# The SBUF layout of an attention and two-MLP kernel: float32r matmul operands moved to the lower 128 KB of each partition

## The chip, the core and the metric

The kernel runs on one core of a Trainium2 chip. The metric is the device time of one execution in microseconds (us). The engines are named as the profile names them: PE (TensorE's matmuls), PEld (its weight loads, which overlap the matmuls), DVE (VectorE), ACT (ScalarE), POOL (GpSimd) and SP (SyncE, which here issues the DMAs; SPq is its queue).

## The reference, cut to what matters

```python
def _attn_ref(q, k, v):                       # (8, 8, 576, 64): batch, head, position, head dim
    q_s = softmax of q over the head dim
    k_s = softmax of k over the positions
    kv = einsum('bhsd,bhse->bhde', k_s, v)
    return einsum('bhsd,bhde->bhse', q_s, kv)

x = attn_out.transpose(0, 2, 1, 3).reshape(4608, 512)
h = x @ w_in1;  x = (h * sigmoid(1.702 h)) @ w_out1      # 512 -> 2048 -> 512, float64 weights
h = x @ w_in2;  x = max(0.01 h, h) @ w_out2              # 512 -> 2048 -> 512
```

The weights arrive as 64-bit floats and are converted on the chip to 32-bit ones.

## The kernel before, in words

The 4608 rows of x are cut into 9 chunks of 512. Each 32-bit operand of an MLP matmul is split into a high part of type float32r and a low part of the same type (what the high part lacks), and a product is the sum of three float32r matmuls: high by high, low by high, high by low. Such a matmul has a stationary operand of 128 x 128 (its weights, loaded by a LDWEIGHTS) and a moving one of 128 x 512. The rows of the trace write a matmul as out<-moving,weights.

- `g1` (L605) computes a block of h directly: moving `x`, weights `wi`, 12 matmuls. It serves chunks 0 and 1 of layer 0, and chunk 8 of both layers (`single`).
- `product` (L618), called from `quad_step`, computes blocks of h for two chunks at once from 7 products in place of 8, 6 matmuls each: moving `x` or `xb` (sums of blocks of x), weights `wa`, `wb`, `wc` or `wd`, outputs `ha`, `hb`, `hc`.
- `g2` (L665) multiplies the activated block by the second weights into four accumulators `acc`: operands `gh`/`gl` (the two parts of the activated block) and `wo`, one moving and the other stationary (exchanged in layer 1), 12 matmuls a block.
- Attention (L390, L400, L421, L476, L500) is plain float32: transposes `kma`, `kmb`, `qtp`, and the matmuls `kvp` and `pxt`. Its 36 units (a chunk and a pair of heads; 32 of them also have a k and v to work on) are dealt out between the matmuls of the MLP, so that there are some 168 short islands of attention on PE.

The program goes: attention of the first units; chunks 0 and 1 with the conversion of layer 0's weights (`c1` to `c4`); `pair_second` for chunk 1; then pairs of chunks (`pair_first`, then `pair_second`), with chunk 8 of each layer by `single`. ACT writes high parts (L80), DVE low parts (L83), DVE also adds the products (L774) and SP issues the DMAs in a fixed order.

Tiles come from pools. A pool stands on one side of the partition (left: counted up from below, right: down from the top), and a pool that is opened later may lie where a released one lay; a tile there waits for the last use of the tile that it replaces. `sb` (attention's tiles, `gf`, `gh`, `gl`, `xr`), `xa` (`x`), `wo` and `c0`/`gb` stand on the left. `first` (raw weights, their conversion, `wi`) stands on the right, and `late` takes its place after chunk 1 (`wa` to `wd`, `xb`, the products' tiles `p1`, `u2`, `v5`, and the conversion of layer 1's weights).

Of the kernel before, what the change touches and what calls it, by code (L numbers as in the profile page):

```python
# [9 lines left out]
F32R = mybir.dt.float32r  # L10
# [16 lines left out]
def tile_softmax_linear_attention_two_mlps(  # L27
# [20 lines left out]
    P = 128  # L48
    T = 512
# [10 lines left out]
    AHEAD = 6  # L60
    LAST = NCH - 1

    sb = ctx.enter_context(tc.tile_pool(name="sb", bufs=1, side="left", reuse_waits="tile"))
    xa = ctx.enter_context(tc.tile_pool(name="xa", bufs=1, side="left", reuse_waits="tile"))
    ps = ctx.enter_context(tc.tile_pool(name="ps", bufs=1, space=bass.MemoryType.PSUM))
    dram = ctx.enter_context(tc.tile_pool(name="dram", bufs=1, space=bass.MemoryType.DRAM))
# [10 lines left out]
    pool = dict(sb=sb, xa=xa)  # L77

    def split_hi(src, hi):
        nc.scalar.copy(hi, src)  # L80
# [182 lines left out]
    def load_wo(i, f):  # L263
        WO[f] = new_wo(f)
        nc.sync.dma_start(out=WO[f].rearrange("p h n -> p (h n)").bitcast(F32), in_=wod[i][f])
# [329 lines left out]
    gb = {}  # L595
# [48 lines left out]
            nc.vector.tensor_tensor(out=t, in0=t, in1=h, op=ALU.max)  # L644

    def halve_hi(f, t):
        gh = sb.tile([P, T], F32R, tag="gh", name="gh", bufs=3)
        gl = sb.tile([P, T], F32R, tag="gl", name="gl", bufs=3)
        split_hi(t, gh)
        g[f] = (t, gh, gl)  # L650

# [36 lines left out]
    def tail(layer, c, acc, between=None):  # L688

        for d in range(KT):  # L690
            for f in range(NF - LAG, NF):
                g2(layer, f, acc, (d,))
            finish(layer, c, acc, d)
            if between and d < len(between):
                between[d]()
# [72 lines left out]
    def quad_step(layer, n, gaps, extra):  # L768
# [24 lines left out]
        act1(layer, a, t11, False)  # L793
        act2(layer, a, t11, False)
        halve_hi(f0, t11)
        run(gaps[4])
        product(b, "s3", W["t3"], False)
# [10 lines left out]
        act1(layer, u2, t12, True)  # L808
        act2(layer, u2, t12, True)
        halve_hi(f1, t12)  # L810
        run(extra[0:1])
        halve_lo(f1)
# [30 lines left out]
    def ready(f):  # L843
        halve_hi(f, gb.pop(f))
        halve_lo(f)
# [31 lines left out]


    pool["wo"] = tc.alloc_tile_pool(name="wo", bufs=1, side="left", reuse_waits="tile")
    first = tc.alloc_tile_pool(name="first", bufs=1, side="right", reuse_waits="tile")  # L880
    pool["cv"] = pool["wi"] = first
    p0 = tc.alloc_tile_pool(name="c0", bufs=1, side="left", reuse_waits="tile")
    places[:] = [1] * 8

    load_first(p0)
# [15 lines left out]
        named[word[:2]](int(word[2:]))  # L901
    p0.release()
    early = False
    pool["gb"] = tc.alloc_tile_pool(name="gb", bufs=1, side="left", reuse_waits="tile")

    def second_x(c, j):
        direct_hi(c, 2, j)
# [80 lines left out]
    blocks = False  # L988
    load_wo(0, 0)
    load_wo(0, 1)  # L990
    first.release()
    late = tc.alloc_tile_pool(name="late", bufs=1, side="right", reuse_waits="tile")
    pool["cv"] = pool["wi"] = pool["xb"] = late
    wi_slots[0] = 5
    late_pools = True

# [153 lines left out]
                    run(items)  # L1150
            held = last
    tail(*held)
    late.release()
    pool["gb"].release()
    pool["wo"].release()


# [28 lines left out]
```

## Time and profile before

| what | value |
|---|---|
| time, median of 3 runs | 1660.8 us (1660.01 to 1662.22) |
| profiled execution: span from first to last instruction | 1657.3 us |
| what a run has beside the span: median less span | 3.5 us |
| PE busy | 1623.3 us, 98% |
| DVE, ACT, POOL busy | 1022.2, 695.4, 27.9 us |
| DMA | 391.55 MB, mean 236 GB/s |
| mean granted TensorE clock | 0.997 of 2.4 GHz |

The profile has no time of its own for the profiled execution beside its span, so the three runs stand for it. The end of a matmul in the trace is modelled and overlaps the start of the next, so that PE's busy time says little about its pace: what a matmul costs is read from the start of one to the start of the next.

### The profile page before, as it was taken

The numbers are of one execution on the slowest core, as the hardware profiler recorded it, in microseconds if no ns is written. First come the engines' busy times: TensorE is split into PE (matmuls) and PEld (weight loads), VectorE is DVE, ScalarE is ACT, GpSimd is POOL, SyncE is SP. The second block draws the span as 40 slices with busy tenths as digits, with TensorE's granted clock in tenths as the row PEclk, the third lists the DMA queues.
The fourth block names the chain that finished last, engine by engine and source line by source line (L and its number), as shares of the span: only waits on it lengthen the run. The fifth ranks groups of instructions, "written<-read, shape, count | busy, mean of one in ns | idle before, by whom it ended". The sixth has DMA issues, their size and how long they took to land.

```text
span 1657.3 us, 22131 instructions
## 1 busy us (share of the span) xinstructions
PE 1623.3 (98%) x7680; PEld 1288.0 (78%) x7680; DVE 1022.2 (62%) x1673; ACT 695.4 (42%) x1582; POOL 27.9 (2%) x162
## 2 busy tenths in 40 slices
PE   5999999999999999999999999999999999999998
PEld 3677777777777778777888888888888888888887
DVE  7899668886767776567435877354735473545222
ACT  8787655665555554444324334211321132112222
POOL 1000000000000000000000000000000000000000
PEclk9999999999999999999999999999999999999999
DMA  7787587778788788778867877665766566657662
GB/s 216 233 275 223 162 263 268 247 258 273 253 270 252 249 279 276 247 250 306 294 213 258 293 274 247 231 214 184 235 231 214 185 230 210 214 184 229 206 203 100
DMA packets 190864, 391.55 MB, mean 236 GB/s; under 512 B 57376, under 2 KB 99360, under 8 KB 190752
## 3 DMA queue, kind: packets, MB, share of 16 engines
q1 hardware_dynamic: 190752, 390.14, 72.2%
q8 instruction: 61, 1.00, 0.2%
q14 instruction: 51, 0.42, 0.1%
HBM read 308.28 MB, written 81.79 MB: 235 GB/s over the span
## 4 chain that ended last, share of the span: by engine, by line
PE 89%; DVE 2%; DMA 2%; issue 2%; ACT 1%; SPq 0%; POOL 0%; ACTq 0%; DVEq 0%; POOLq 0%
PE acc L665 44%; PE hb L618 14%; PE ha L618 10%; PE hc L618 9%; PE h L605 8%; PE pxt L500 2%; DMA o<-cv 1%; PE kvp L421 1%; PE qtp L476 1%; DMA wo<-wo 1%; DMA raw<-in_moe_w_in_dram 1%; DVE gl L83 0%; DVE cv L121 0%; DVE kt L406 0%; DMA w<-cv 0%
## 5 line engine op out<-in xcount | busy, mean ns | idle before, releaser
L665 PE MATMUL acc<-gh,wo 128*128 128x512 f32 x1152 | 363.7, 396 | 5.2 <-DMA wo<-wo 3.4
L665 PE MATMUL acc<-wo,gh 128*128 128x512 f32 x1152 | 355.7, 390 | 0.0
L665 PEld LDWEIGHTS acc<-wo,gh 128*128 128x128 f32 x1152 | 216.2, 188 | 46.4 <-issue 0.2
L665 PEld LDWEIGHTS acc<-gh,wo 128*128 128x128 f32 x1152 | 211.5, 188 | 51.4 <-issue 5.2
L665 PE MATMUL acc<-gl,wo 128*128 128x512 f32 x576 | 225.7, 392 | 0.0
L665 PE MATMUL acc<-wo,gl 128*128 128x512 f32 x576 | 225.2, 391 | 0.0
L605 PE MATMUL h<-x,wi 128*128 128x512 f32 x768 | 194.7, 403 | 2.8 <-ACT wi L80 2.8
L605 PEld LDWEIGHTS h<-x,wi 128*128 128x128 f32 x768 | 144.2, 190 | 41.4 <-ACT wi L80 4.5
L83 DVE TENSOR_TENSOR gl<-gb,gh 128x512 fp32r<-128x512 f32 x128 | 87.7, 689 | 124.2 <-ACT gh L80 123.8
L618 PE MATMUL ha<-x,wa 128*128 128x512 f32 x624 | 164.0, 398 | 0.0
L80 ACT CAST gh<-gf 128x512 fp32r<-128x512 f32 x160 | 98.9, 618 | 137.5 <-PE acc L665 66.9
L83 DVE TENSOR_TENSOR gl<-gf,gh 128x512 fp32r<-128x512 f32 x160 | 110.3, 690 | 65.0 <-ACT gh L80 63.3
L80 ACT CAST gh<-gb 128x512 fp32r<-128x512 f32 x128 | 79.2, 621 | 161.9 <-PE acc L665 161.4
L618 PEld LDWEIGHTS ha<-x,wa 128*128 128x128 f32 x624 | 115.7, 187 | 32.9 <-issue 5.0
L665 PEld LDWEIGHTS acc<-gl,wo 128*128 128x128 f32 x576 | 108.3, 188 | 24.7 <-issue 1.0
L665 PEld LDWEIGHTS acc<-wo,gl 128*128 128x128 f32 x576 | 108.1, 188 | 23.6
L774 DVE TENSOR_TENSOR u<-hb,p 128x512 f32<-128x512 f32 x56 | 38.6, 689 | 133.6 <-PE hb L618 117.9
L618 PE MATMUL hb<-x,wc 128*128 128x512 f32 x384 | 100.1, 395 | 0.0
L452 ACT ACTIVATE qt<-qt,qmx 128x64 f32<-128x64 f32 x256 | 86.1, 339 | 14.8 <-DVE qmx L442 14.4
L618 PE MATMUL hb<-xb,wb 128*128 128x512 f32 x336 | 87.0, 394 | 0.0
L618 PEld LDWEIGHTS hb<-x,wc 128*128 128x128 f32 x384 | 72.0, 187 | 17.3
L779 ACT COPY p<-ha 128x512 f32<-128x512 f32 x56 | 32.7, 584 | 117.3 <-PE ha L618 117.2
(125 smaller groups left out, 2076.9 us busy)
## 6 DMA issues: line engine op xcount, KB each, us to landing
wo<-wo SPq DMA_DIRECT2D x288, 512.0 KB, 4.2
wa<-wq SPq DMA_DIRECT2D x40, 512.0 KB, 4.1
wb<-wq SPq DMA_DIRECT2D x40, 512.0 KB, 4.6
wc<-wq SPq DMA_DIRECT2D x40, 512.0 KB, 4.7
raw<-in_moe_w_in_dram SPq DMA_DIRECT2D x32, 512.0 KB, 4.9
raw<-in_moe_w_out_dram SPq DMA_DIRECT2D x32, 512.0 KB, 5.1
wi<-wq SPq DMA_DIRECT2D x32, 512.0 KB, 4.5
wd<-wq SPq DMA_DIRECT2D x40, 256.0 KB, 3.4
```

Of the source, the lines that this page charges most:

```text
L80: nc.scalar.copy(hi, src)
L83: nc.vector.tensor_tensor(out=lo, in0=src, in1=hi.bitcast(F32), op=ALU.subtract)
L421: nc.tensor.matmul(pk[h * D : (h + 1) * D, 0 : D + 1], rest[0][:, h, :] if r == R and rest else km[:, h, r, :], vm[:, h, r, :] if r < R el ...
L452: nc.scalar.activation(t[:, h, r, :], t[:, h, r, :], AF.Exp, bias=mx[:, h, r : r + 1], accum_out=sm[:, h, r : r + 1],)
L476: nc.tensor.transpose(pt[:, r * P : (r + 1) * P], qs[:, r, :, :].rearrange("p h d -> p (h d)"), ident)
L500: nc.tensor.matmul(pv[o, :, a:e], kvb[b, j][o, :], t[o, :, a:e], start=True, stop=True)
L605: nc.tensor.matmul(h, WI[f][:, b, wh, o * P : (o + 1) * P], xs[f"a{side}{b + 1}"][xh][:, o, :], start=(i == 0), stop=(i == n - 1),)
L618: nc.tensor.matmul(h, w[:, wh, o * P : (o + 1) * P], xo[xh][:, o, :], start=(start and i == 0), stop=(i == 5), skip_group_check=not start,)
L665: nc.tensor.matmul(acc[d], lhsT, rhs, start=(f == 0 and i == 0), stop=(f == NF - 1 and i == 2))
L774: add = lambda out, h, t: nc.vector.tensor_tensor(out=out, in0=h, in1=t, op=ALU.add)
L779: nc.scalar.copy(p1, a)
```

## The change

No instruction is added or removed, and no tile's size or number of buffers changes. What changes is where the tiles lie:

| tiles | read by PE as | KB in the partition before | after |
|---|---|---|---|
| `gh`, `gl` | float32r | 47 to 59 | 16 to 28 |
| `x` | float32r | 75 to 107 | 28 to 60 |
| `wo` | float32r | 107 to 123 | 60 to 76 |
| `wi`, first part (8 buffers) | float32r weights | 184 to 216 | 76 to 108 |
| `wa` to `wd`, `wi`, later (5 buffers) | float32r weights | 168 to 188 | 76 to 96 |
| `xb` | float32r moving | 188 to 212 | 96 to 120 |
| raw weights and their conversion (8 buffers) | not read | 160 to 184 and 216 to 224 | 108 to 140 |
| `p1`, `u2`, `v5` | not read | 212 to 224 | 128 to 140 |
| `gb` (and attention's first inputs) | first inputs: float32 | 123 to 155 | 145 to 177 |
| attention's tiles | float32 | 16 to 41 | 177 to 202 |
| `gf`, `xr` | not read | 41 to 47, 59 to 75 | 202 to 224 |

```diff
-    sb = ctx.enter_context(tc.tile_pool(name="sb", bufs=1, side="left", reuse_waits="tile"))
+    sb = ctx.enter_context(tc.tile_pool(name="sb", bufs=1, side="right", reuse_waits="tile"))
+    lo = ctx.enter_context(tc.tile_pool(name="lo", bufs=1, side="left", reuse_waits="tile"))
...
     def halve_hi(f, t):
-        gh = sb.tile([P, T], F32R, tag="gh", name="gh", bufs=3)
-        gl = sb.tile([P, T], F32R, tag="gl", name="gl", bufs=3)
+        gh = lo.tile([P, T], F32R, tag="gh", name="gh", bufs=3)
+        gl = lo.tile([P, T], F32R, tag="gl", name="gl", bufs=3)
...
-    first = tc.alloc_tile_pool(name="first", bufs=1, side="right", reuse_waits="tile")
-    pool["cv"] = pool["wi"] = first
-    p0 = tc.alloc_tile_pool(name="c0", bufs=1, side="left", reuse_waits="tile")
+    pool["wi"] = tc.alloc_tile_pool(name="wi", bufs=1, side="left", reuse_waits="tile")
+    pool["cv"] = tc.alloc_tile_pool(name="first", bufs=1, side="left", reuse_waits="tile")
+    p0 = tc.alloc_tile_pool(name="c0", bufs=1, side="right", reuse_waits="tile")
...
-    pool["gb"] = tc.alloc_tile_pool(name="gb", bufs=1, side="left", reuse_waits="tile")
+    pool["gb"] = tc.alloc_tile_pool(name="gb", bufs=1, side="right", reuse_waits="tile")
...
-    first.release()
-    late = tc.alloc_tile_pool(name="late", bufs=1, side="right", reuse_waits="tile")
-    pool["cv"] = pool["wi"] = pool["xb"] = late
+    pool["cv"].release()
+    pool["wi"].release()
+    for name in ("wi", "xb", "cv"):
+        pool[name] = tc.alloc_tile_pool(name="late_" + name, bufs=1, side="left", reuse_waits="tile")
```

Since the later pools replace other tiles than before, the order of instructions differs in one place, at the passage from chunk 1's first half to the pairs; PE's order differs there by one exchange of neighbours. SP's queue at the load of the first block of weights for the pairs (`w`, L214 before and L215 after; `wo<-` are loads of the second weights, `wo_15<-wo` is the store of the last converted ones, `vt` and `qt` are attention's inputs), before:

```order
L303 DMA vt<-in_v_dram 128x4x64 x2
L306 DMA vt<-in_v_dram 64x2x64
L214 DMA w_2476<-w_0_123 128x1024
L265 DMA wo<-wo_4_95 128x1024
L241 DMA wq_0_75<-wa 128x1024
L265 DMA wo<-wo_5_96 128x1024
```

and after:

```order
L316 DMA qt<-in_q_dram 80x2x256
L266 DMA wo<-wo_0_94 128x1024
L172 DMA wo_15_109<-wo 128x1024
L215 DMA w_2489<-w_0_126 128x1024
L266 DMA wo<-wo_1_95 128x1024
L316 DMA qt<-in_q_dram 48x2x256
```

The load moves ahead, from behind the third and fourth `wo` load to directly behind the last store of converted weights. On DVE, the sums `t` that are made from this block (L221 to L223 before), before the change:

```order
L640 SCALAR_TENSOR_TENSOR gb<-gb,h 128x512
L462 RECIPROCAL qsm<-qsm 128x8
L395 TENSOR_REDUCE km<-kma 128x1
L221 TENSOR_TENSOR t_2547<-w_2476 128x2x256
L83 TENSOR_TENSOR gl<-gb,gh 128x512
L222 TENSOR_TENSOR t_2547<-w_2476,t_2547 128x256
L83 TENSOR_TENSOR wa<-w_2476,wa 128x2x256
```

and after:

```order
L463 RECIPROCAL qsm<-qsm 128x8
L641 SCALAR_TENSOR_TENSOR gf<-gf,h 128x512
L222 TENSOR_TENSOR t_2560<-w_2489 128x2x256
L223 TENSOR_TENSOR t_2560<-w_2489,t_2560 128x256
L84 TENSOR_TENSOR gl<-gf,gh 128x512
L224 TENSOR_TENSOR t_2560<-w_2489,t_2560 128x256
L465 TENSOR_TENSOR qs<-qt,qsm 128x2x4x64
```

The first sums now stand ahead of `gl<-gf,gh`, the low part of chunk 0's last block. On ACT, the casts of the first weights `wa` to `wd`, before:

```order
L452 ACTIVATE qt,qsm<-qt,qmx 128x64 x5
L80 CAST gh<-gb 128x512
L80 CAST wa<-w_2476 128x2x256
L80 CAST wd<-w_2476 128x2x256
L80 CAST wb<-t_2547 128x2x256
L80 CAST gh<-gb 128x512
L80 CAST wc<-t_2547 128x2x256
```

and after:

```order
L81 CAST wa<-w_2489 128x2x256
L532 COPY xr<-pxt 128x512
L81 CAST wd<-w_2489 128x2x256
L81 CAST wb<-t_2560 128x2x256
L81 CAST wc<-t_2560 128x2x256
L453 ACTIVATE qt,qsm<-qt,qmx 128x64
L81 CAST gh<-gb 128x512
```

All four casts now stand ahead of a `gh<-gb` that stood ahead of them or between them.

## Rows read from the trace of the kernel before

**Rows 1.** The page: span, and the chain that ended last by engine.

```profile
span 1657.3 us, 22131 instructions
PE 89%; DVE 2%; DMA 2%; issue 2%; ACT 1%; SPq 0%; POOL 0%; ACTq 0%; DVEq 0%; POOLq 0%
```

**Rows 2.** Windows: us, busy and count of each engine, clock, DMA share, GB/s.

```profile
20.00:60.00 40.00, 32.27 (x195) 20.50 (x193) 34.16 (x70) 30.93 (x90) 2.00 (x11) 0.91 0.69 213
100.00:200.00 100.00, 99.46 (x534) 75.17 (x533) 83.55 (x162) 73.59 (x194) 4.47 (x26) 1.00 0.71 225
800.00:1000.00 200.00, 200.00 (x870) 162.93 (x869) 121.31 (x197) 72.28 (x121) 0.00 (x0) 1.00 0.76 261
```

**Rows 3.** PE's timeline: start, length, line, out<-moving,weights, shapes, count; layer 1's end.

```profile
1581.32 2.95 PE L605 MATMUL h<-x,wi 128*128 128x512 f32 x12
1584.11 0.61 PE L665 MATMUL acc<-wo,gh 128*128 128x512 f32 x2
...
1586.84 2.95 PE L605 MATMUL h<-x,wi 128*128 128x512 f32 x12
```

**Rows 4.** PE's timeline, a pair step of layer 1.

```profile
1000.72 0.62 PE L665 MATMUL acc<-wo,gh 128*128 128x512 f32 x2
...
1003.48 1.56 PE L618 MATMUL ha<-x,wa 128*128 128x512 f32 x6
1004.88 1.55 PE L618 MATMUL hb<-xb,wb 128*128 128x512 f32 x6
1006.27 1.53 PE L618 MATMUL hc<-xb,wb 128*128 128x512 f32 x6
1007.64 1.52 PE L618 MATMUL ha<-xb,wa 128*128 128x512 f32 x6
1009.00 1.33 PE L618 MATMUL hb<-x,wc 128*128 128x512 f32 x5
```

**Rows 5.** Windows, the whole span, instructions that touch tile x.

```profile
0.00:1657.30 1657.30, 537.23 (x2112) 393.88 (x2112) 44.19 (x40) 37.62 (x40) 1.00 0.73 236
```

**Rows 6.** The same for tile xb.

```profile
0.00:1657.30 1657.30, 250.08 (x1008) 188.12 (x1008) 25.13 (x21) 21.44 (x21) 1.00 0.73 236
```

**Rows 7.** The same for the accumulators acc.

```profile
0.00:1657.30 1657.30, 824.50 (x3456) 643.32 (x3456) 24.73 (x36) 21.43 (x36) 1.00 0.73 236
```

**Rows 8.** PE's timeline, a long run of g2 behind an island of attention.

```profile
237.65 1.08 PE L500 MATMUL pxt<-qT,kv 64*64 64x192 f32 x8
...
238.99 0.63 PE L665 MATMUL acc<-gh,wo 128*128 128x512 f32 x2
...
241.53 0.39 PE L665 MATMUL acc<-gl,wo 128*128 128x512 f32 x1
...
242.89 0.39 PE L665 MATMUL acc<-gl,wo 128*128 128x512 f32 x1
```

**Rows 9.** The page's groups, DVE's low parts: count, busy, mean ns, idle before.

```profile
L83 DVE TENSOR_TENSOR gl<-gb,gh 128x512 fp32r<-128x512 f32 x128 | 87.7, 689 | 124.2 <-ACT gh L80 123.8
L83 DVE TENSOR_TENSOR gl<-gf,gh 128x512 fp32r<-128x512 f32 x160 | 110.3, 690 | 65.0 <-ACT gh L80 63.3
```

**Rows 10.** PE's waits: us in total, times, longest.

```profile
PE acc L665 <- DMA wo<-wo: 3.4, 1, 3.4
```

**Rows 11.** Timelines of SP, ACT, DVE and PE around the first weights of the pairs.

```profile
179.11 0.69 DVE L83 TENSOR_TENSOR gl<-gf,gh 128x512 fp32r<-128x512 f32 x1 [0.77 <-ACT gh L80]
184.38 0.39 PE L665 MATMUL acc<-gl,wo 128*128 128x512 f32 x1
209.16 0.59 SPq L214 DMA_DIRECT2D w<-w  x1
213.53 0.62 ACT L80 CAST wa<-w 128x512 fp32r<-128x512 f32 x1
213.76 0.68 DVE L221 TENSOR_TENSOR t<-w 128x512 f32<-128x512 f32 x1
254.01 1.56 PE L618 MATMUL ha<-x,wa 128*128 128x512 f32 x6
```

More of the change, by code (lines that the diff above doesn't have):

```diff
@@ L1152, in tile_softmax_linear_attention_two_mlps @@
     tail(*held)
-    late.release()
     pool["gb"].release()
-    pool["wo"].release()
+    for name in ("cv", "xb", "wi", "wo"):
+        pool[name].release()
 _INS = ['q', 'k', 'v', 'moe_w_in', 'moe_w_out', 'moe2_w_in', 'moe2_w_out']
```

## The prediction

> **What bounds the kernel now.** I read the page first: the chain that ended last is PE for 89% of the span, and no other engine has more than 2% of it [rows 1]. Then the windows by stretch: from 100 us on PE has hardly a gap (99.46 of 100 us, later 200.00 of 200 us) at a granted clock of 1.00, while DVE, ACT and the DMA engines have room; only the first 100 us, at 0.91 in the stretch shown, leave PE idle [rows 2]. So nothing that this change can hide or uncover on another engine matters, unless it makes PE wait; what matters is PE's pace. The pace is the time from the start of one matmul to the start of the next, and the reader finds it in PE's timeline by subtracting starts and dividing by the count.
>
> There the same kind of matmul (float32r, 512 columns) has two paces. At the end of layer 1, twelve `h<-x,wi` take 1584.11 - 1581.32 = 2.79 us, 232.5 ns each, and the twelve of `acc` behind them 1586.84 - 1584.11 = 2.73 us, 227.5 ns each [rows 3]. In a pair step six `ha<-x,wa` take 1.40 us (233.3 ns) and six `ha<-xb,wa` 1.36 us (226.7 ns): the same line, the same output, the same weight tile; only the moving tile differs [rows 4]. By the table of places, `x` lies at 75 to 107 KB and `wa` at 168 to 188 KB, `xb` at 188 to 212 KB. So `x` by `wa` has its two operands on different sides of some border between 123 and 168 KB, while `xb` by `wa` has both above it, and `acc` (`gh`, `gl` at 47 to 59 KB, `wo` at 107 to 123 KB) both below. The fast pace is that of operands on one side, whichever, and the slow one that of operands on two sides. Nearness explains it no better: `gh` and `wo` lie 48 to 76 KB apart and are fast.
>
> There is also an after-effect. Six `hb<-xb,wb`, both operands above but behind a slow group, take 1.39 us; `hc<-xb,wb` behind them takes 1.37 and the next `ha<-xb,wa` 1.36 [rows 4]. A long run of `acc` behind an island of attention needs 241.53 - 238.99 = 2.54 us for its first eleven full matmuls (230.9 ns), and then 1.36 us for six (226.7 ns) [rows 8]. So a disturbance is paid for over some ten matmuls, and 226.7 ns is what a run settles at.
>
> **The change part by part.** It puts every float32r operand of PE below 124 KB. I cost this against 226.7 ns.
>
> Moving operand `x`, weights above: 2112 matmuls [rows 5]. Of these, `g1` has 768 (4 passes of 16 blocks of 12); at 232.5 ns [rows 3] each saves 5.8 ns, 4.5 us. The other 1344 are products at 233.3 ns [rows 4], 6.6 ns each, 8.9 us. Together 13.4 us.
>
> Moving operand `xb`: 1008 matmuls, 168 sixes [rows 6]. These are on one side already and gain only the after-effect: some 104 `hb` sixes 1.39 - 1.36 = 0.03 us each, the other 64 about 0.01 us [rows 4], together 3.7 us.
>
> `acc`: 3456 matmuls, 288 twelves [rows 7]. Their operands move from one place below to another. In the pair steps a twelve takes 1003.48 - 1000.72 = 2.76 us, against 12 x 226.7 = 2.72 us; 7 pairs x 8 steps x 2 = 112 of them give 4.5 us [rows 4]. The 64 twelves between `g1` groups take 2.73 us [rows 3] and give 0.6 us. The 112 in `pair_second` run in one piece and give nothing. Together 5.1 us.
>
> The sum of what can be won is 13.4 + 3.7 + 5.1 = 22.2 us. From it go three things. First, attention's islands stay: each of 168 leaves an after-effect behind it, between nothing and 2.54 - 11 x 0.2267 = 0.046 us [rows 8], so 0 to 7.7 us. That row is one of the long after-effects, so I take 0.025 us, 4.2 us. Second, attention's operands now lie above and the MLP's below, so that the last matmul ahead of an island runs while weights from the other side are loaded, and perhaps the first behind it too. The trace has no such neighbours; below, it costs nothing (part of these borders were crossed before), above, 2 x 6.6 ns x 168 = 2.2 us; I take one side, 1.1 us. Third, in the first 100 us PE waits for others; the part of the gain that falls there, about 0.5 us, I count as lost. That leaves 22.2 - 4.2 - 1.1 - 0.5 = 16.4 us.
>
> Attention's own matmuls had both operands below and now have both above: 0. DVE and ACT: a low part `gl` reads `gf` (below) in 690 ns and `gb` (mostly above) in 689 ns, writing below [rows 9], so place is nothing to DVE, and I take the same for ACT and DMA.
>
> The new order at the passage to the pairs: the first block of weights was loaded at 209.16 us, reached DVE at 213.76 and was needed by PE at 254.01 [rows 11], so loading it some 35 us earlier brings nothing. It can cost: DVE now meets the first two sums ahead of `gl<-gf,gh`, which ended at 179.80 and was first read at 184.38, 4.6 us later [rows 11]. Two sums of at most 0.7 us, or even a wait of a whole landing (213.76 - 209.16 = 4.6 us), fit into that. Without this cover, `acc` would wait up to 4.6 us. I take 0. The four casts ahead of a `gh` on ACT delay it by 4 x 0.62 = 2.5 us [rows 11], less what they jump; the same bound holds, and I take 0. PE's stall of 3.4 us for a `wo` load [rows 10] has nothing to do with places and stays.
>
> By the Trainium skill ("TensorE: Matmul & The Clock Gate", section "Wait — 56ns, not 53.3ns?") warm matmuls follow each other by the columns over 2.4 GHz plus about 2.5 ns, which is 215.7 ns here, whatever the operands' place. The trace does not agree: it shows 226.7 and 233.3 ns. By the page the change would bring 0, by the rows 16.4 us.
>
> The profiled span is 1657.3 us and the median run 3.5 us longer; nothing outside the span changes. 1657.3 - 16.4 = 1640.9 us of span, **1644.4 us** of time.
>
> **The rivals.**
>
> *No change, 1660.8 us.* The two paces could belong to the kind of group and its neighbours, not to place: `hb<-xb,wb` is on one side and slow on average. Against it speaks `ha<-x,wa` beside `ha<-xb,wa` [rows 4], with one weight tile and 6.6 ns between them. The Trainium skill ("SBUF — State Buffer", section "Who interferes with whom") says "PE and ACT never wait on anyone", by which place would change nothing; the two paces in the rows above speak against that. Chance 0.08.
>
> *The direct part alone, about 1650 us.* The pace of `x` by low weights falls as forecast (13.4 us), but the after-effects stay, as if they came from each change of group and not from the slow groups ahead: then neither `xb` nor `acc` gains, the islands are as they are, and with the borders at their upper bound 13.4 - 2.2 - 0.5 = 10.7 us are left. For it: an island on one side leaves an after-effect too [rows 8]. Against it: twelve `acc` behind `g1` show hardly one [rows 3]. It would show in `acc` groups behind products at 2.76 us still. Chance 0.10.
>
> *Slower, about 1672 us.* All that PE reads, and all that DMA, ACT and DVE write for it (weights, `xb`, `gh`, `gl`), now shares the lower half; if that is a common resource, every matmul slows. Were all 6300 or so float32r neighbours at the 1.39 / 6 = 231.7 ns of the `hb` group, against the present mean of about 230 ns (200 us / 870 [rows 2]), it would be 6300 x 1.8 = 11 us more. It decides from a settled pace of about 230.5 ns up. Against it: `acc` shares the lower half with its own loads and casts already, and settles at 226.7 ns [rows 8] while the DMA engines are busy. Chance 0.04.
>
> **How the numbers follow.** The forecast has a chance of 0.78, with a range of its own from 22.2 - 0.5 = 21.7 us (1639 us) to 22.2 - 7.7 - 2.2 - 0.5 = 11.8 us (1649 us). To hold 8 in 10 with the small terms open (a wait of 4.6 us at the passage, a shifted `wo` stall of 3.4 us) I go to 1638 and 1654 us. About 0.2%, 3.3 us, is what a measurement of this kernel can tell from no change: faster 0.88 (the forecast and the direct part alone), same 0.08, slower 0.04.
>
> **What would show it.** In the profile after: six `ha<-x,wa` in 1.36 to 1.37 us, twelve `h<-x,wi` in 2.72 to 2.73, twelve `acc` behind a product in 2.72 to 2.74, and some 880 matmuls where 800 to 1000 us had 870. Wrong would be: `h<-x,wi` still at 2.79 us (place is not it), or a fast pace with new gaps on PE between 170 and 260 us (the passage), or `acc` slower than before (a crowded lower half).

## The result and the profile after

The changed kernel takes 1646.56 us (median of 5 runs, 1642.35 to 1649.66) against 1661.33 us (median of 5, 1660.01 to 1662.22): a ratio of 0.9911, 95% interval 0.9896 to 0.9925, 14.8 us less. The profiled execution is the fastest of the five, 1642.35 us, with 1.75 us around its span (every run listed has 1.7 to 1.9 us there, not 3.5). The page's span and the chain by engine:

```profile
span 1640.6 us, 22126 instructions
PE 85%; DMA 4%; DVE 4%; issue 2%; ACT 1%; SPq 0%; ACTq 0%; POOL 0%; DVEq 0%
```

PE still bounds the kernel, and the span is 16.7 us shorter than in [rows 1]. The page counts 22126 instructions against 22131; those of PE, PEld, DVE, ACT and POOL are as many as before. The same stretches as in [rows 2] (us, then busy time and count of PE, PEld, DVE, ACT, POOL, then clock, DMA share, GB/s):

```profile
20.00:60.00 40.00, 33.13 (x200) 20.59 (x201) 35.20 (x74) 31.64 (x93) 2.00 (x11) 0.96 0.70 216
100.00:200.00 100.00, 99.16 (x541) 75.87 (x541) 84.33 (x164) 74.26 (x199) 4.92 (x26) 1.00 0.75 232
800.00:1000.00 200.00, 200.00 (x884) 165.60 (x883) 122.44 (x200) 73.36 (x122) 0.00 (x0) 1.00 0.77 267
```

In the 200 us from 800 us on there is room for 884 matmuls where 870 stood, with PE's busy time and the clock as they were and the other engines hardly changed. In the stretch from 20 to 60 us the granted clock is 0.96 in place of 0.91; more on that below. PE's timeline at the end of layer 1, which answers to [rows 3]:

```profile
1570.95 2.88 PE L606 MATMUL h<-x,wi 128*128 128x512 f32 x12
1573.67 0.62 PE L666 MATMUL acc<-wo,gh 128*128 128x512 f32 x2
...
1576.39 2.88 PE L606 MATMUL h<-x,wi 128*128 128x512 f32 x12
```

Both twelves now take 2.72 us. And the pair step, which answers to [rows 4]:

```profile
992.68 0.61 PE L666 MATMUL acc<-wo,gh 128*128 128x512 f32 x2
...
995.40 1.52 PE L619 MATMUL ha<-x,wa 128*128 128x512 f32 x6
996.76 1.52 PE L619 MATMUL hb<-xb,wb 128*128 128x512 f32 x6
998.12 1.52 PE L619 MATMUL hc<-xb,wb 128*128 128x512 f32 x6
999.48 1.52 PE L619 MATMUL ha<-xb,wa 128*128 128x512 f32 x6
1000.84 1.52 PE L619 MATMUL hb<-x,wc 128*128 128x512 f32 x6
```

Every six takes 1.36 us, and the twelve `acc` 2.72: there is one pace, 226.7 ns, where there were two and an after-effect. So the gain is where it was forecast. Whether it came for the reason that was given is another question, and the experiments answer it with no.

### The profile page after: what moved, and what is told of

The parts are those of the page before. It is cut to its first block, busy times and chain, and to the rows that moved or that the text cites. A ratio compares the mean times of both kernels' runs of the same rounds, so it can differ in the third digit from the quotient of the medians.

```text
span 1640.6 us, 22126 instructions
## 1 busy us (share of the span) xinstructions
PE 1606.8 (98%) x7680; PEld 1287.8 (78%) x7680; DVE 1020.4 (62%) x1673; ACT 694.4 (42%) x1582; POOL 27.1 (2%) x162
## 4 chain that ended last, share of the span: by engine, by line
PE 85%; DMA 4%; DVE 4%; issue 2%; ACT 1%; SPq 0%; ACTq 0%; POOL 0%; DVEq 0%
PE acc L666 43%; PE hb L619 13%; PE ha L619 9%; PE hc L619 9%; PE h L606 7%; PE pxt L501 2%; DMA w<-cv 2%; DMA o<-cv 1%; PE kvp L422 1%; DVE cv L122 1%; DMA qt<-in_q_dram 1%; PE qtp L477 1%; DVE gl L84 1%; DMA raw<-in_moe_w_in_dram 1%; DVE cv L112 0%
## 5 line engine op out<-in xcount | busy, mean ns | idle before, releaser
L606 PE MATMUL h<-x,wi 128*128 128x512 f32 x768 | 189.2, 396 | 2.8 <-ACT wi L81 2.8
L619 PE MATMUL ha<-x,wa 128*128 128x512 f32 x624 | 160.6, 393 | 0.0
```

Of the source, the lines that this page charges most:

```text
L606: nc.tensor.matmul(h, WI[f][:, b, wh, o * P : (o + 1) * P], xs[f"a{side}{b + 1}"][xh][:, o, :], start=(i == 0), stop=(i == n - 1),)
L619: nc.tensor.matmul(h, w[:, wh, o * P : (o + 1) * P], xo[xh][:, o, :], start=(start and i == 0), stop=(i == 5), skip_group_check=not start,)
```

## Experiments

**Places alone.** A small kernel without attention and MLP runs nothing but float32r matmuls, in series of 24 that each read one moving place and one place of weights, all starts at whole multiples of 256 bytes (shortened):

```python
MOVING = (20, 44, 76, 100, 116, 126, 127, 128, 140, 160, 190, 216)        # KB
WEIGHTS = (24, 60, 92, 120, 127.5, 127.75, 128, 136, 150, 170, 200)       # KB
for w in WEIGHTS:
    for m in MOVING:
        24 x matmul(acc, weights at w, moving at m)      # in two halves of 12, pa/pb or pc/pd
```

> No attention and no MLP: only float32r matmuls of 128 x 512 on constant data, in series of 24 that each read one moving place and one place of weights (132 pairs of places), and eight series that alternate two pairs of places. Theory (two sides of 128 KB; what counts is the moving operand of one matmul against the weights that are loaded beside it, which are those of the next): settled pace 226.7 ns for every pair of places on one side, however far apart, 233 to 235 ns for every pair on two sides, however near; moving operands that end at 128 KB count as below. In the alternating series (below, below) and (above, above) the pace is slow in every second interval or both although each matmul has both operands on one side, and in (below, above) and (above, below) it is fast. Rival (distance between operands): the pace depends on the distance, 126 beside 128 KB is fast and 20 beside 200 KB slow even on one side. Rival (a matmul's own pair counts): the alternating series come out the other way round. Rival (not place): one pace for all.

PE's timeline (start, length, line, out and operands, count): both halves of moving 20 by weights at 24 KB (the first two rows); the second half of moving 160 and the first of moving 190, by weights at 24 KB (the next two); and the second half of moving 44 and the first of moving 76, by weights at 170 KB (the last two):

```profile
39.06 2.88 PE L42 MATMUL pa<-buf 128*128 128x512 f32 x12
41.78 2.88 PE L42 MATMUL pb<-buf 128*128 128x512 f32 x12
...
90.74 2.88 PE L42 MATMUL pd<-buf 128*128 128x512 f32 x12
93.46 2.88 PE L42 MATMUL pa<-buf 128*128 128x512 f32 x12
...
634.74 2.88 PE L42 MATMUL pd<-buf 128*128 128x512 f32 x12
637.46 2.88 PE L42 MATMUL pa<-buf 128*128 128x512 f32 x12
```

Twelve take 2.72 us from start to start everywhere, in all 132 pairs of places (226.6 to 226.8 ns), and so in the alternating series. The theory of two sides falls here: below and above 128 KB together cost nothing.

**Weights and xb across the border, in the kernel.** Two kernels stack the changed kernel's pools in another order, so that some buffers of the weights, or of `xb`, lie above 128 KB:

```diff
-    for name in ("wi", "xb", "cv"):          # changed kernel
+    for name in ("cv", "xb", "wi"):          # weights_across (and wi above the conversion at first)
+    for name in ("wi", "cv", "xb"):          # xb_across
```

> The changed kernel with the pools of one side stacked in another order, so that the first-layer weights lie at 120 to 140 KB (five buffers, two below and three above 128 KB; at first eight buffers at 108 to 140 KB, three above) and all else float32r below 120 KB. Theory: matmuls whose weights lie above cost 233.3 ns, the others 226.7; about 0.6 x 2352 products, 0.6 x 384 and 0.375 x 384 direct ones, some 1790 x 6.6 ns = 11.8 us, and 3 to 5 us of after-effects: span 1655 to 1659 us against 1640.6. In the rows, groups of one kind split by the place of their weight tile. Rival (the border lies elsewhere between 123 and 168 KB, at 140 or above): no change, 1640.6; (it lies at 124): four of five buffers slow, span about 1661.

> The changed kernel with the moving operand xb at 116 to 140 KB (six buffers, three below and three above 128 KB), all else float32r below. Theory: the other direction, a moving operand above and weights below, costs as much: half of 1008 matmuls x 6.6 to 8.3 ns = 3.3 to 4.2 us and 1 to 2 us of after-effects, span 1645 to 1647 us against 1640.6. Rival (only weights above with a moving operand below are slow): 1640.6, and xb groups all at 1.36 us for six.

Measured: ratios to the kernel before of 0.9909 (0.9883 to 0.9935) for `weights_across` and 0.9901 (0.9885 to 0.9918) for `xb_across`, spans 1644.6 and 1641.7 us; both keep the gain. In `weights_across` the sixteen blocks of layer 1's last chunk go through all five buffers of the weights, three of them above 128 KB, and from 1558.6 us on each of the fourteen groups of twelve `h<-x,wi` takes 2.72 us. One of them:

```profile
1574.96 2.88 PE L606 MATMUL h<-x,wi 128*128 128x512 f32 x12
1577.68 0.62 PE L666 MATMUL acc<-wo,gh 128*128 128x512 f32 x2
```

In `xb_across` the first three rows read two buffers of `xb` each, so that they cover all six, three of which lie above 128 KB:

```profile
997.79 1.52 PE L619 MATMUL hb<-xb,wb 128*128 128x512 f32 x6
999.15 1.52 PE L619 MATMUL hc<-xb,wb 128*128 128x512 f32 x6
1000.51 1.52 PE L619 MATMUL ha<-xb,wa 128*128 128x512 f32 x6
1001.87 1.30 PE L619 MATMUL hb<-x,wc 128*128 128x512 f32 x5
```

Each six takes 1.36 us. Both runs miss what the theory of two sides forecast (spans of 1655 to 1659 us and of 1645 to 1647 us): it fails for weights above and for a moving operand above.

**gh and gl above.**

```diff
-    lo = ctx.enter_context(tc.tile_pool(name="lo", bufs=1, side="left", reuse_waits="tile"))
+    lo = ctx.enter_context(tc.tile_pool(name="lo", bufs=1, side="right", reuse_waits="tile"))
```

> The changed kernel with gh and gl alone above 128 KB (165 to 177 KB); x, xb, wo and the first-layer weights below. These matmuls (acc, 3456 of them) were fast in both kernels so far. Theory: all cross now, 3456 x 6.6 ns = 22.8 us and up to 5 us of after-effects in the products behind them: span 1663 to 1669 us, slower than the kernel before; twelve acc take 2.80 us in place of 2.72. Rival (acc is fast by its kind, not by its place): 1640.6.

Measured: 1.0014 (1.0000 to 1.0029), span 1660.5 us, somewhat less than the 1663 to 1669 of the theory: the gain is gone. PE's timeline:

```profile
1581.56 0.63 PE L666 MATMUL acc<-wo,gh 128*128 128x512 f32 x2
...
1584.35 2.89 PE L606 MATMUL h<-x,wi 128*128 128x512 f32 x12
1587.08 0.63 PE L666 MATMUL acc<-wo,gh 128*128 128x512 f32 x2
```

Now the twelve `acc` take 2.79 us and the `h<-x,wi` 2.73: the slow pace has moved to the other kind of matmul. That is what two sides would do, and yet the first three runs say that sides do nothing. What the slow cases share is finer. The right side of the partition is filled from a top that is no round number, so its tiles start at odd places. These starts are worked out from the sizes of the pools' tiles; no trace shows an address. In the kernel before, `x` starts at 75 KB exactly (0 past a multiple of 256 bytes) and `wa` at 167.96875 KB (224 past one); in `g_above`, `wo` starts at 48.125 KB (128 past) and `gh` at 165.09375 KB (96 past). In `weights_across` and `xb_across` all float32r operands were stacked from below and start 128 past a multiple of 256, as in the changed kernel; and `xb` by `wa` before were both 224 past. The new theory: the pace depends on whether moving operand and weights start alike within a small block, not on the side.

**Starts alone.** The small kernel again, with places fixed and starts shifted by 0 to 256 bytes (12 moving by 12 weights, both below 128 KB; a smaller set with the weights above):

> Only float32r matmuls of 128 x 512 on constant data, series of 24, operands in the same regions but their starts shifted by 0 to 256 bytes: 12 starts of the moving operand by 12 of the weights with both below 128 KB, 4 by 4 with the weights above 128 KB, then six alternating series. New theory (what the earlier runs have in common is not the side of 128 KB but the start of an operand within a line of 64 bytes: in the kernel before, x starts at a multiple of 64 and the weights for it 32 bytes past one): a series is slow, 233 to 235 ns, where moving operand and weights differ by 32 bytes modulo 64 and fast, 226.7, where they agree modulo 64, on either side of 128 KB; what counts is the weights of the next matmul, so that (0,0),(0,32) alternate between slow and fast, (0,0),(32,32) are slow both times and (0,32),(32,0) fast both times. What 4, 8, 16 and 24 bytes do is open. Rival (modulus 128 or more): 64 beside 0 is slow as well. Rival (the start matters for one operand alone): rows or columns of the map are slow as a whole. Rival (neither side nor start; traffic of other engines makes the pace): one pace of 226.7 for all.

The settled pace in ns (the mean of the last 12 intervals within each 24, from PE's starts), a part of the map, moving start across, weights' start down:

```
weights\moving   0      32      64     128     160     256   (bytes)
       0       226.7   233.3   228.8   233.3   234.3   226.7
      32       233.3   226.7   233.3   233.3   233.3   233.3
      64       233.3   233.3   226.7   228.9   233.3   233.3
     128       231.7   234.6   233.3   226.7   233.3   232.8
     160       233.3   233.3   234.2   233.3   226.7   233.3
     256       226.7   233.3   228.9   233.3   234.3   226.7
weights above 128 KB:
       0       226.7   233.3   228.9
      32       233.3   226.7   233.3
      64       233.3   233.3   226.7
```

PE's timeline for weights at 0: the second half at moving 0 (the first row), at moving 32 (the third), at moving 64 (the fifth); then moving 16 by weights at 4 (the seventh), both at 16 (the ninth) and both at 32 (the eleventh). The row behind each shows where the twelve end:

```profile
41.38 2.88 PE L40 MATMUL pb<-buf 128*128 128x512 f32 x12
44.10 3.00 PE L40 MATMUL pc<-buf 128*128 128x512 f32 x12
...
69.32 2.96 PE L40 MATMUL pd<-buf 128*128 128x512 f32 x12
72.12 2.96 PE L40 MATMUL pa<-buf 128*128 128x512 f32 x12
...
80.47 2.91 PE L40 MATMUL pd<-buf 128*128 128x512 f32 x12
83.22 2.97 PE L40 MATMUL pa<-buf 128*128 128x512 f32 x12
...
125.09 2.88 PE L40 MATMUL pd<-buf 128*128 128x512 f32 x12
127.81 2.98 PE L40 MATMUL pa<-buf 128*128 128x512 f32 x12
...
259.00 2.96 PE L40 MATMUL pd<-buf 128*128 128x512 f32 x12
261.80 2.96 PE L40 MATMUL pa<-buf 128*128 128x512 f32 x12
...
403.81 2.88 PE L40 MATMUL pd<-buf 128*128 128x512 f32 x12
406.53 1.78 PE L40 MATMUL pa<-buf 128*128 128x512 f32 x7
```

These take 2.72, 2.80, 2.75, 2.72, 2.80 and 2.72 us. The rule that I had stated (modulo 64) is wrong, the kind of rule is right, as long as both starts are multiples of 32 bytes: of the 49 such pairs with both below 128 KB, the nine that are equal modulo 256 run at 226.7 ns, the five with the moving operand 64 bytes past the weights at 228.8 to 228.9 ns (a half-way case), and the other 35 at 231.7 to 234.6 ns. Since 0 and 256 count as equal and 64 and 128 do not, the period that fits the map is 256 bytes.

With a start that is no multiple of 32 bytes the rule fails. Equal starts are then slow (both at 4, 8, 16, 24 or 48 bytes: 230.0 to 237.8 ns), some unequal ones are fast (moving 16 by weights at 4: 226.7 ns), and the slowest pair of the map is moving 4 by weights at 32, with 240 ns. What orders these was not found. All float32r tiles of the kernels here start at multiples of 32 bytes. The alternating series gave mixed paces (230 ns for (0,32),(32,0), 231.7 for (0,0),(32,32)), so which neighbour's weights count is not settled.

**32 or 128 bytes, in the changed kernel.** An empty tile below the first-layer weights shifts them and `xb`, and nothing else that PE reads as float32r; all float32r operands stay below 124 KB and the order of PE's instructions does not change (the lines that release the pad are left out):

```diff
+    pad = tc.alloc_tile_pool(name="pad", bufs=1, side="left")
+    pad.tile([P, 8], F32, tag="pad", name="pad")      # 32 bytes; [P, 32] is 128 bytes
     pool["wi"] = tc.alloc_tile_pool(name="wi", bufs=1, side="left", reuse_waits="tile")
```

> The changed kernel with 32 bytes left empty below the first-layer weights, so that these, xb and what lies above them start 32 bytes past a multiple of 64, and gh, gl, x and wo at a multiple; every float32r operand stays below 124 KB. Theory of the start within 64 bytes: the pattern of the kernel before returns, twelve h<-x,wi in 2.79 us, six ha<-x,wa in 1.40, six xb groups that are not behind a slow one in 1.36, acc behind a product 2.75; span about 1657 us against 1640.6. Theory of the two sides of 128 KB: nothing changes, 1640.6 us.

> The changed kernel with 128 bytes left empty below the first-layer weights: x, gh, gl, wo start 128 past a multiple of 256, wi to wd and xb at one. Order as in the changed kernel. Theory of modulo 256: the slow pace returns as with 32 bytes (in the map 128 beside 0 gives 231.7 to 233.3 ns), span 1653 to 1657 us. Rival (modulo 64 or 128): 1640.6 us.

Measured: 0.9994 (0.9981 to 1.0006), span 1653.9 us, with 32 bytes; 0.9991 (0.9981 to 1.0001), span 1656.0 us, with 128. Either pad loses the gain. The timeline with 32 bytes:

```profile
1577.80 2.96 PE L606 MATMUL h<-x,wi 128*128 128x512 f32 x12
1580.59 0.62 PE L666 MATMUL acc<-wo,gh 128*128 128x512 f32 x2
...
1583.32 0.86 PE L606 MATMUL h<-x,wi 128*128 128x512 f32 x3
```

and with 128:

```profile
1579.64 2.96 PE L606 MATMUL h<-x,wi 128*128 128x512 f32 x12
1582.43 0.62 PE L666 MATMUL acc<-wo,gh 128*128 128x512 f32 x2
```

`h<-x,wi` takes 2.79 us in both, the value of [rows 3].

**224 or 32 bytes, in the kernel before.** The other direction: every tile stays on its old side, and a pad at the top moves the right side's tiles:

```diff
+    pad = ctx.enter_context(tc.tile_pool(name="pad", bufs=1, side="right"))
+    pad.tile([P, 56], F32, tag="pad", name="pad")     # 224 bytes; [P, 8] is 32 bytes
```

> The kernel before, every tile on its old side, with 224 bytes left empty at the top, so that the tiles of the right side lie 224 bytes lower: x, wo, gh and gl as well as wi, wa to wd and xb now start at multiples of 256 bytes; the order of instructions is that of the kernel before. Theory (starts of moving operand and weights must agree modulo 256 bytes): the whole gain without the new layout, twelve h<-x,wi in 2.72 us, six ha<-x,wa in 1.36, span 1640 to 1643 us. Theory of the two sides of 128 KB: as before, 1657 us. It also tells what the new order of instructions was worth: with it 1640.6 in one look.

> The same with 32 bytes: the right side's tiles start at a multiple of 64 bytes, but 192 past a multiple of 256 (64 before the next), against 0 for x. Theory of modulo 256: not the whole gain; in the map the pair with the moving operand 64 past the weights settles at 228.9 ns, so h<-x,wi twelve in about 2.75 us, 2112 x 2.2 ns = 4.6 us and some after-effects short of the full gain, span 1645 to 1650 us. Rival (modulo 64 is enough): 1640 to 1643 us. Rival (two sides of 128 KB): 1657 us.

> The changed kernel itself, beside before_pad224 on the same chip. Theory of the starts: the two take the same time within 2 us, since both have all starts equal modulo 256 bytes; the sides of 128 KB and the changed order of instructions at the passage to the pairs are worth nothing. Rival (part of the gain comes from the sides): the changed kernel is faster by more than 3 us.

Measured: with 224 bytes 0.9900 (0.9884 to 0.9916), span 1638.5 us; with 32 bytes 0.9955 (0.9941 to 0.9970), span 1648.3 us; the changed kernel beside them on the same chip 0.9914 (0.9899 to 0.9928), span 1642.1 us. The timeline with 224 bytes:

```profile
1574.36 2.88 PE L607 MATMUL h<-x,wi 128*128 128x512 f32 x12
1577.08 0.62 PE L667 MATMUL acc<-wo,gh 128*128 128x512 f32 x2
...
1579.80 2.43 PE L607 MATMUL h<-x,wi 128*128 128x512 f32 x10
```

and with 32:

```profile
1578.41 2.91 PE L607 MATMUL h<-x,wi 128*128 128x512 f32 x12
1581.15 0.61 PE L667 MATMUL acc<-wo,gh 128*128 128x512 f32 x2
```

With 224 bytes, `x` by `wi` crosses 128 KB as before and takes 2.72 us. With 32 the starts agree modulo 64 but not modulo 256 (`x` 64 past the weights), and it takes 2.74: the half-way case of the map, in the kernel. Two lines give what the new layout gives; the intervals of `before_pad224` and `after_again` overlap (medians 1643.3 and 1644.08 us; the profiled spans are 3.6 us apart), and neither is shown to be faster.

## Why the prediction was right, and where its reason was wrong

**The step that failed** is the sentence that `x` by `wa` is slow because its operands lie "on different sides of some border between 123 and 168 KB". The rows had sorted the pairs rightly into fast and slow, and in the kernel before the two explanations sort them alike, because left-side tiles start at 0 modulo 256 and right-side tiles at 224: any pair on two sides of 128 KB also differs in its start, with `xb` by `wa` and `acc` on one side and equal. Nothing in that trace could tell them apart; the table of places, with its fractions of a KB cut off, hid the other reading. That the number came out is luck as far as the reason goes, because the change happens to do both: it moves the operands below 128 KB and, by stacking them all from below, gives them one start modulo 256. The runs separate the two: operands on two sides with equal starts keep or bring the gain (`weights_across`, `xb_across`, `before_pad224`), and operands on one side with unequal starts lose it (`after_off32`, `after_off128`). Why unequal starts cost some 6.6 ns a matmul is not shown.

**The terms.** The paces came as forecast. `h<-x,wi` went from 2.79 to 2.72 us for twelve and `ha<-x,wa` from 1.40 to 1.36 for six; `hb<-xb` went from 1.39 to 1.36 and the pair steps' `acc` from 2.76 to 2.72, so the after-effects went with the slow groups, and the rival by which only the direct part comes is refuted by these rows. The sum over all float32r neighbours from 100 us on, each interval less 226.7 ns and without the first one behind an island, is some 21 us before and 4 us after. The difference of 17.1 us stands against 16.4 predicted. What is left lies almost wholly in the ten intervals that follow the first one behind an island (3.7 us). There the forecast (168 islands at 0.025 us, 4.2 us) is near by two errors that cancel: the trace has 139 islands, some 120 of them from 100 us on, and each leaves 0.03 us. The borders (1.1 us) cost nothing that shows: the last interval ahead of a `kma`, `kmb` or `qtp` island has a median of 230 to 231 ns before and 227 to 230 after, and the first behind an island is on average 2 ns shorter after.

**The new order at the passage** cost nothing that shows, as taken: PE is busy 99.16 us of 100 to 200 us against 99.46, and `before_pad224`, in the old order, has the same time as the changed kernel within the intervals. The stall for a `wo` load became 2.0 us from 3.4 in [rows 10], and yet nothing was won by it in the profiled run:

```profile
769.54 0.98 PE L666 MATMUL acc<-gh,wo 128*128 128x512 f32 x2 [2.01 <-DMA wo<-wo]
...
770.74 1.05 PE L666 MATMUL acc<-gh,wo 128*128 128x512 f32 x2
...
772.02 1.05 PE L666 MATMUL acc<-gh,wo 128*128 128x512 f32 x2
```

After the stall the granted clock fell to the lower of its two levels, 1.2 GHz (the window from 770 to 772 us):

```profile
770.00:772.00 2.00, 2.00 (x6) 1.55 (x5) 2.00 (x3) 0.00 (x0) 0.00 (x0) 0.50 0.84 340
```

Three matmuls took 772.02 - 770.74 = 1.28 us, 427 ns each. Seven had this pace, and with the first and the last of the stretch they cost some 1.7 us more than at 226.7 ns. Behind the longer stall of the kernel before the clock stayed at 1.00 (776 to 778 us).

**The time** fell by 14.8 us in the medians, 1.6 us less than predicted. The spans fell by 16.7 us, which looks like the 16.4 of the forecast, but this compares two single executions, and that of the changed kernel is the fastest of its five, 4.2 us below their median. Part of it comes from a stretch in which the forecast counted nothing. The same five `acc` matmuls behind a wait at about 100 us start as follows, in the kernel before, in the changed kernel and in `after_again`:

```profile
99.61 1.67 PE L665 MATMUL acc<-gh,wo 128*128 128x512 f32 x5 [1.80 <-ACT wo L80]
98.00 1.76 PE L666 MATMUL acc<-gh,wo 128*128 128x512 f32 x5 [1.81 <-ACT wo L81]
99.81 1.77 PE L666 MATMUL acc<-gh,wo 128*128 128x512 f32 x5 [1.80 <-ACT wo L81]
```

The changed kernel is 1.6 us ahead there, at a granted clock of 0.96 from 20 to 60 us; `after_again` is the same kernel, had 0.91 as the kernel before, and is 0.2 us behind. So that lead is scatter, and the changed layout is worth some 15 us in the spans too (1657.3 less 1642.1 of `after_again` is 15.2). The 3.5 us that were put around the span were the distance of one execution's span from the median of others; they stand on both sides of the forecast and explain no miss. The rest lies within the scatter of the runs, 1642.35 to 1649.66 us; what makes them scatter was not studied.

**The other rivals.** No change: refuted by the ratio. A crowded lower half: refuted, since with everything below the pace is 226.7 ns. That is the fastest settled pace in every run here, also in the small kernels, where no other engine computes beside the matmuls. The Trainium skill ("TensorE: Matmul & The Clock Gate", section "Wait — 56ns, not 53.3ns?") gives a rule by which it would be 215.7 ns; no run here meets it.

## What to carry to other kernels

Where PE is full and float32r matmuls differ by a few per cent in pace, look at the byte at which moving operand and weights start, modulo 256, before anything larger: a pad of 224 bytes was worth 1% here. Let both start at a multiple of 32 bytes as well; the map shows equal starts that are slow without it. Tiles that are stacked from one end share their start as long as every tile's size is a multiple of 256 bytes; a pool at the other end, or one small tile among them, breaks that. And when two properties change together, a forecast that comes true proves neither: here a pad that changes one of them cost two lines and decided it.

## What the runs showed of the hardware that was not expected

- Float32r matmuls of 128 x 512 follow each other at 226.7 ns when the moving operand and the weights start at multiples of 32 bytes that are equal modulo 256, at 228.8 to 228.9 ns with the moving operand 64 bytes past the weights, and at 231.7 to 234.6 ns for the other starts tried that are multiples of 32 (`map_of_offsets`). With starts that are no multiples of 32 equal ones are slow too (230.0 to 237.8 ns). Where in the partition the two lie makes no difference (`map_of_pace`, 132 pairs of places, 226.6 to 226.8 ns).
- After an island the pace settles only over about ten matmuls [rows 8]; behind a slow series of the small kernel a fast one settles within eight at most. Why was not tried.
- A wait of 2.0 us on PE was followed by matmuls at 427 ns at a granted clock of 0.50 in the changed kernel; one of 3.4 us in the kernel before was not.
